# Attention and a two-layer network on one core: the first batch in two blocks of 384 tokens, and a planner that counts VectorE's reads of its own last result

## The chip, the cores and the metric

The kernel runs on one core of a Trainium2 chip. The metric is the device time of one execution in microseconds (us); several executions are timed and their median is given. One further execution is recorded by the profiler. The engines are TensorE (PE), VectorE (DVE), ScalarE (ACT), GpSimd (POOL) and SyncE (SP), which issues the DMAs. Each runs its own instructions in the order in which they stand in the program and waits for the others at semaphores.

## The reference

```python
# q, k, v: (4 batches, 8 heads, 768 positions, 64); 8 global keys, a local window of 96
scores = scale * np.matmul(q, k.transpose(0, 1, 3, 2)) + bias   # bias falls with the distance, by head
scores = np.where(is_global | is_local, scores, -1e9)
a = softmax(scores)                                             # with 1e-9 added to the sum
x = np.matmul(a, v)                                             # -> 3072 tokens x 512
h = x @ w_in                                                    # 512 x 2048
out = (h * np.cos(h)) @ w_out                                   # 2048 x 512
```

All of q, k and v are float32; the two weights are float64 and come as pairs of 32-bit words that the kernel turns into two float32 parts, a high one and a rest.

## The kernel before, in words

Attention goes by blocks of 96 queries (R), which need 96 + 104 keys each. The 8 blocks of a batch are taken as chunks of 3, 3 and 2 (BLOCKS), so there are 12 chunks in all. A chunk has four units, one for each pair of heads. A unit's scores are made on PE (line 632 in plain float32 for the first 8 units, which the code calls exact; line 636 from a high part and a rest, split on ACT, POOL and DVE, for the others), masked and reduced on DVE (fold, line 654; least, line 663), put through exp on ACT (line 688), scaled (lines 712 and 717), turned on PE (line 803), copied out of PSUM with two masks (lines 814 and 820), and multiplied with v (line 846). The result is split into xh and xl (lines 269, 271 and 893).

The network goes by chunks m of 256 tokens (MW). A step is one chunk with two of the 16 slices f of 128 hidden columns: m1 (line 909, function moe1) makes 128 x 256 of h for each slice, so that one elementwise pass is 512 wide: turns on ACT (927), angle on DVE (930), cosine on ACT (933), product on DVE (966), then high (269) and rest (977). m2 multiplies with w_out about 2.6 steps later: chunks 0 to 3 plainly (line 922, moe2), chunks 4 to 11 (m of FAST or more) with seven instead of eight products (line 1071), whose sums of g are four DVE or POOL instructions in one piece of work (lines 1017 to 1020). The weights are decoded once, slice by slice, while the first chunks run (lines 407 to 438; wjoin is 428, the rest is 438). PHASES says how far the first chunk goes before the second one starts.

The order on every engine is made by a planner (class Plan): every piece of work is an op with a cost on each engine that may do it, a due time, and the buffers it uses (named places of which each class has a few); the planner walks through time, takes the op that is due first of those that are ready, and the instructions are written in that order. WEIGHT and HURRY say how dear an engine counts when an op may go to several. Where PE would stand idle early on, emit puts in matmuls on zeros (line 1354).

Of the kernel before, what the change touches and what calls it, by code (L numbers as in the profile page):

```python
# [28 lines left out]
WIN = R + SLOT  # L29
BLOCKS = ((0, 1, 2), (3, 4, 5), (6, 7))  # L30
CT = 3
CW = CT * R
MW = 256
# [3 lines left out]
QK = KW + CW  # L37
BIG = 1.0e30
# [7 lines left out]
PERIOD = 6800  # L46
LAG = 2.6
MARGIN, EACH = 1.9, 1.7
# [6 lines left out]
NT, NST, NPV, NX, NV, NRAW, NQK, NRR, NG, NS, NOO = 4, 3, 3, 3, 3, 3, 2, 3, 2, 2, 2  # L55

EXACT = 8
FAST = 4
SUMS = -8

DIFFER = tuple(range(4, 12))
BEFORE = {0: 1000, 1: 10000, 2: -5000}
WLEAD = -2500
SLACK = 350
TAIL = 0.3
# [20 lines left out]
class Op:  # L86
    def __init__(self, engines, emit, after, uses, due, table, extra, port, mode):
        self.engines, self.emit, self.uses, self.due, self.table = engines, emit, uses, due, table
        self.extra, self.port, self.mode = extra, port, mode
        self.slack = 0  # L90
        self.after = [a for a in after if a is not None]
        self.then = []
        self.left = len(self.after)
        self.ready = 0
        self.start = None


class Plan:
# [6 lines left out]
    TABLE = 1300  # L105
    AHEAD = 5000
    SWITCH = 200

    def __init__(self, places, free):
        self.ops = []  # L110
        self.places = {c: list(v) for c, v in places.items()}
        self.busy = {}
        self.free = dict(free)
        self.port = 0
        self.mode = None

# [21 lines left out]
    def run(self):  # L138
# [19 lines left out]
        while todo:  # L158
# [5 lines left out]
            while again:  # L164
                again = False
                for e, f in self.free.items():
# [7 lines left out]
                    holds = lambda o, x: x == POOL or (x == DVE and o.port)  # L174
                    for o in ready[e]:
                        if o.ready > t or (best is not None and o.key >= best.key):
                            continue
# [18 lines left out]
                        if ok:  # L196
                            best = o
# [13 lines left out]
                    d = o.engines[e]  # L211
                    if e == ACT and o.table and o.table != table:
# [35 lines left out]
class Net:  # L248
    def __init__(self, ctx, tc, qk, qt, kt, v, lim, w_in, w_out, out):
        self.tc, self.nc = tc, tc.nc  # L250
        self.qk, self.v, self.w_in, self.w_out, self.out = qk, v, w_in, w_out, out
        self.qt, self.kt = qt, kt
        self.lims = lim
        self.B, self.NCH, self.H, self.D, _ = qk.shape
        self.S = v.shape[1]
        self.DF, self.DM = w_out.shape
        self.NP = self.H // 2
# [114 lines left out]
    def plan_weights(self, f):  # L372
# [5 lines left out]
        first = next(s for s, x in enumerate(self.seq) if x[1] == f // 2)  # L378
        wi = int(first * PERIOD) - WLEAD
        wo = int((first + LAG) * PERIOD) - WLEAD  # L380
# [69 lines left out]
    def plan_combined(self, q):  # L450
# [4 lines left out]
        due = int((next(s for s, x in enumerate(self.seq) if x[0] == FAST) + q + SUMS) * PERIOD)  # L455
# [62 lines left out]
    def plan_loads(self, n, b2):  # L518
# [3 lines left out]
        b, c = divmod(n, self.NCH)  # L522
        W = 2 * UB * D
        nb = len(BLOCKS[c])
        t0 = BLOCKS[c][0] * R
        lead = 1 if c == 0 else 0
        vs = Slot("v", lambda i: self.work.tile([SLOT, 1 + CT, W], F32, name="v", tag=i))
        L = dict(n=n, first=c == 0, v=vs, nb=nb)
        src = self.v[b][:, b2 * W : (b2 + 1) * W]
        nt = 1 + nb - lead  # L530
        s = t0 - (1 - lead) * R

        def blocks(e):
            nc.sync.dma_start(vs.tile[:R, lead : lead + nt], src[s : s + nt * R].rearrange("(t p) d -> p t d", p=R))

        def glob(e):
            nc.sync.dma_start(
                vs.tile[R:, lead:nb], src[:G].rearrange("p (t d) -> p t d", t=1).broadcast_to([G, nb - lead, W])
# [21 lines left out]
    def plan_unit(self, L, pr):  # L560
# [7 lines left out]
        b, c = divmod(n, self.NCH)  # L568
        u["hs"] = slice((pr % UB) * P, (pr % UB + 1) * P)
        att = u["att"] = "early" if n == 0 else "wide" if n <= FAST else "att"  # L570
        exact = self.order.index(n) * self.NP + pr < EXACT
# [3 lines left out]
        row = lambda: Slot("raw", lambda i: self.work.tile([P, QK], F32, name="raw", tag=i))  # L575
        if exact:
            raw = row()
            src = self.qk[b, c, 2 * pr : 2 * pr + 2].rearrange("j p w -> (j p) w")

            def load(e):  # L580
                nc.sync.dma_start(raw.tile[:, k0 : KW + wq], src[:, k0 : KW + wq])

            def queries(e):
                x = raw.tile[:, KW : KW + wq]
# [5 lines left out]
            o = p.op({SP: 470}, load, [], [raw], extra=1422 * (KW + wq - k0) // 1000)  # L590
# [3 lines left out]
        else:  # L594
            heads = [
                self.plan_split(row(), self.qk[b, c, 2 * pr + j], k0, k1, wq, self.steepness(2 * pr + j))
                for j in range(2)
# [20 lines left out]
        for job in jobs:  # L618
# [3 lines left out]
            def score(e, pss=pss):  # L622
                for i in range(len(pss[0][1])):
                    for ps, items in pss:
# [5 lines left out]
                        if exact:  # L630
                            z = raw.tile[j * D : (j + 1) * D]
                            nc.tensor.matmul(out, z[:, KW:][:, q0], z[:, k : k + w], start=True, stop=True)
# [91 lines left out]
    def plan_split(self, raw, src, k0, k1, wq, sc):  # L724

        nc, p, D = self.nc, self.plan, self.D
        qk = Slot("qk", lambda i: [
            self.work.tile([P, 2, CW], F32R, name="qs", tag=f"q{i}"),
            self.work.tile([P, KW], F32R, name="ks", tag=f"k{i}"),
        ])  # L730

        def load(e, a):
            nc.sync.dma_start(raw.tile[a : a + D, k0 : KW + wq], src[:, k0 : KW + wq])

        def qhigh(e):
            nc.scalar.activation(qk.tile[0][:, 0, :wq], raw.tile[:, KW : KW + wq], AF.Copy, scale=sc)

        def qrest(e):
            qs = qk.tile[0]
            nc.vector.scalar_tensor_tensor(  # L740
                qs[:, 1, :wq], raw.tile[:, KW : KW + wq], sc, qs.bitcast(F32)[:, 0, :wq],
# [12 lines left out]
        loads = [p.op({SP: 470}, lambda e, a=a: load(e, a), [], [raw], extra=711 * (KW + wq - k0) // 1000) for a in (0, D)]  # L754
# [7 lines left out]
        k = p.op({DVE: 70 + w * 535 // 512, POOL: 100 + w * 1125 // 512}, krest, [k], [raw, qk], port=True)  # L762
        return qk, [q, k]

    def plan_values(self, u):
        nc, p, D = self.nc, self.plan, self.D
        n, pr, hs, vs, tt, nb = u["n"], u["pr"], u["hs"], u["v"], u["tt"], u["nb"]
# [70 lines left out]
        def av(e):  # L838
            for t in range(nb):
                pv = pvs[t // 2].tile  # L840
                lead = u["first"] and t == 0
                for c in (1,) if lead else (0, 1):
                    k = R if c else SLOT
                    for j in range(2):
# [3 lines left out]
                            (vd.tile[:, off + t] if c and not lead and differ else vs.tile[:k, t + c, hs])[:, j * D : (j + 1) * D],  # L848
# [21 lines left out]
        s0 = BLOCKS[n % self.NCH][0] * R  # L870
        for n, pr, _, _, _, off in units:
            s, e = s0, s0 + nb * R
            while s < e:
                c = s // MW
                self.plan_x(n, pr, n - n % self.NCH + c, s - c * MW, px, s - s0 + off * R, min(e, (c + 1) * MW) - s, done)
                s = min(e, (c + 1) * MW)

    def plan_x(self, n, pr, m, at, px, c0, w, done):

        nc, p = self.nc, self.plan  # L880
        if m not in self.x:
            self.x[m] = Slot("x", lambda i: [
                self.work.tile([P, self.NP, MW], F32R, name=nm, tag=f"{nm}{i}") for nm in ("xh", "xl")
            ])
        x = self.x[m]
        a, c = slice(at, at + w), slice(c0, c0 + w)

        def high(e):
            self.copy(e, x.tile[0][:, pr, a], px.tile[:, c])

        def rest(e):
            xh, xl = x.tile
            nc.vector.tensor_tensor(xl[:, pr, a], px.tile[:, c], xh.bitcast(F32)[:, pr, a], op=ALU.subtract)  # L893

        o = self.chain("xh", p.op({ACT: 50 + w * 427 // 512, DVE: 70 + w * 535 // 512}, high, [done], [px, x]))
        self.xdone.setdefault((m, pr), []).append(
            p.op({DVE: 70 + w * 535 // 512}, rest, [o], [px, x], due=self.xdue(n, pr)))

    def xdue(self, n, pr):
        rest = self.NP - 1 - pr  # L900
        first = next(s for s, x in enumerate(self.seq) if x[0] == n)
        if n in EARLY:
            return first * PERIOD - BEFORE[n] - rest * EARLY[n]
        return int((first - MARGIN - rest * EACH) * PERIOD)
# [30 lines left out]
    def plan_step(self, s, m, q, a, b):  # L935

        nc, p = self.nc, self.plan
        due = s * PERIOD
        x = self.x[m]
# [486 lines left out]
```

## Time and profile before

| | before |
|---|---|
| median of 3 runs (lowest to highest) | 693.3 us (692.57 to 694.97) |
| the profiled execution: its time | 693.8 us |
| its span, first to last instruction | 691.9 us |
| PE, DVE, ACT, POOL busy, share of the span | 97%, 83%, 76%, 47% |
| granted TensorE clock, mean | 0.987 |

The profiled execution is 1.9 us longer than its span, which is time around the first and last instruction. Busy time of PE is modelled and holds waits in part, so a PE that is busy 97% need not be at its peak: the pace of its matmuls tells more.

### The profile page before, as it was taken

The page shows a single profiled execution, that of the slowest core. Times are in us where ns is not written, and L with a number is a line of the kernel's source. Part 1 is how long each engine was busy: PE and PEld are TensorE (multiplying, and loading weights), DVE is VectorE, ACT ScalarE, POOL GpSimd, SP SyncE. Part 2 cuts the span into 40 slices and gives each one's busy share as a digit, 9 for nine tenths or more (in the row PEclk, how much of TensorE's full clock was granted, in tenths as well). Part 3 has the DMA queues.
Part 4 walks back from the last instruction along what each step waited for, and adds up shares of the span by engine and source line. Part 5 has one row for each costly group of instructions (what it writes and reads, how often), then busy time and mean ns, then how long its engine had stood idle before and what let it go on. Part 6 is the DMA issues. An engine that isn't in the chain of part 4 may idle for free.

```text
span 691.9 us, 17874 instructions
## 1 busy us (share of the span) xinstructions
PE 668.4 (97%) x5979; PEld 627.0 (91%) x5979; DVE 574.5 (83%) x1813; ACT 525.9 (76%) x1311; POOL 322.5 (47%) x463
## 2 busy tenths in 40 slices
PE   6998999999999999999999999999999999999995
PEld 3677899889999999999999989999999989999995
DVE  6899998999889898888987887877987787887764
ACT  6899997887878868768878877666887786875442
POOL 6682434453445535415455665562545665630200
PEclk8899999999999999999999999999999999999998
DMA  8999000443546666776777767776877966665664
GB/s 290 286 359 347 29 1 1 130 129 115 194 142 200 196 205 202 219 220 213 243 237 219 222 194 216 240 235 220 241 219 218 265 196 203 200 214 182 216 196 157
DMA packets 88053, 138.56 MB, mean 200 GB/s; under 512 B 10256, under 2 KB 34704, under 8 KB 87952
## 3 DMA queue, kind: packets, MB, share of 16 engines
q1 hardware_dynamic: 87952, 137.32, 64.1%
q8 instruction: 50, 0.82, 0.5%
q14 instruction: 51, 0.42, 0.2%
HBM read 120.51 MB, written 16.78 MB: 198 GB/s over the span
## 4 chain that ended last, share of the span: by engine, by line
PE 38%; DVE 24%; ACT 16%; issue 5%; POOL 5%; DMA 2%; SPq 0%; POOLq 0%; DVEq 0%; ACTq 0%
PE bank L909 17%; PE bank L1071 10%; PE bank L922 5%; ACT tt L688 3%; DVE rr L966 2%; PE bank L846 2%; PE bank L636 2%; DVE tt L663 2%; DVE rr L930 2%; ACT rr L933 2%; DVE qs L740 2%; DVE bank L654 2%; ACT sh L269 1%; DVE gl L977 1%; DVE sl L1026 1%
## 5 line engine op out<-in xcount | busy, mean ns | idle before, releaser
L909 PE MATMUL bank<-xh,w 128*128 128x256 f32 x1536 | 329.2, 285 | 0.8 <-DVE rr L966 0.4
L909 PEld LDWEIGHTS bank<-xh,w 128*128 128x128 f32 x1536 | 257.9, 189 | 7.8 <-DVE rr L966 1.6
L909 PE MATMUL bank<-xl,w 128*128 128x256 f32 x768 | 215.2, 280 | 0.0
L909 PEld LDWEIGHTS bank<-xl,w 128*128 128x128 f32 x768 | 145.3, 189 | 2.2 <-DVE xl L893 0.2
L688 ACT ACTIVATE tt<-tt,st 96x104 f32<-96x104 f32 (+1 forms) x256 | 94.6, 371 | 6.4 <-DVE st L663 5.7
L933 ACT ACTIVATE rr<-rr,half_pi 128x512 f32<-128x512 f32 x96 | 69.4, 723 | 28.8 <-DVE rr L930 28.0
L966 DVE TENSOR_TENSOR rr<-bank,rr 128x512 f32<-128x512 f32 x96 | 66.0, 688 | 29.3 <-ACT rr L933 28.9
L922 PE MATMUL bank<-w,gh 128*128 128x256 f32 (+1 forms) x384 | 87.9, 322 | 2.5 <-DVE w L438 1.4
L717 POOL TENSOR_TENSOR tt<-tt,st 96x416 f32<-96x416 f32 (+1 forms) x64 | 45.0, 710 | 77.3 <-DVE qs L740 30.1
L269 ACT CAST gh<-rr 128x384 fp32r<-128x384 f32 (+1 forms) x86 | 46.9, 545 | 40.5 <-DVE rr L966 26.9
L930 DVE SCALAR_TENSOR_TENSOR rr<-rr,bank 128x512 f32<-128x512 int32 x96 | 65.3, 680 | 11.6 <-ACT rr L927 11.1
L1071 PE MATMUL bank<-ws,sh 128*128 128x256 f32 x384 | 72.9, 284 | 0.2
L927 ACT ACTIVATE rr<-bank 128x512 int32<-128x512 f32 x96 | 56.6, 589 | 16.3 <-PE bank L909 15.9
L922 PEld LDWEIGHTS bank<-w,gh 128*128 128x128 f32 x384 | 58.9, 188 | 5.1 <-DVE w L438 2.6
L922 PE MATMUL bank<-w,gl 128*128 128x256 f32 (+1 forms) x192 | 60.9, 317 | 0.0
L636 PE MATMUL bank<-ks,qs 128*96 128x200 f32 (+1 forms) x416 | 56.3, 259 | 3.9 <-DVE st L663 3.1
L269 ACT CAST sh<-sf 128x512 fp32r<-128x512 f32 x57 | 35.4, 620 | 31.0 <-DVE sf L1020 17.0
L1071 PEld LDWEIGHTS bank<-ws,sh 128*128 128x128 f32 x384 | 58.2, 188 | 0.8 <-DVE oo L1089 0.6
L663 DVE CUSTOM_DVE_ANT_0 tt<-bank,dd 96x104 f32<-96x104 f32 (+1 forms) x256 | 56.4, 257 | 2.9
L636 PEld LDWEIGHTS bank<-ks,qs 128*96 128x96 f32 x416 | 46.8, 162 | 8.9 <-issue 5.0
L1071 PE MATMUL bank<-ws,sl 128*128 128x256 f32 x192 | 53.5, 279 | 0.0
L1071 PE MATMUL bank<-w,gh 128*128 128x256 f32 x256 | 48.5, 281 | 0.0
(132 smaller groups left out, 1595.5 us busy)
## 6 DMA issues: line engine op xcount, KB each, us to landing
ws<-sum SPq DMA_DIRECT2D x256, 256.0 KB
raw<-in_qk_dram SPq DMA_DIRECT2D x64, 150.0 KB
raw<-in_qk_dram SPq DMA_DIRECT2D x48, 174.0 KB
raw<-in_w_in_dram SPq DMA_DIRECT2D x16, 512.0 KB
sum<-sw SPq DMA_DIRECT2D x64, 128.0 KB
raw<-in_qk_dram SPq DMA_DIRECT2D x48, 148.0 KB
out_dram<-oo SPq DMA_DIRECT2D x24, 256.0 KB
v<-in_v_dram SPq DMA_DIRECT2D x32, 144.0 KB
```

The source lines that it names most:

```text
L269: self.nc.scalar.copy(out, x)
L636: nc.tensor.matmul(out, qs[:, m, q0], ks[:, k : k + w], start=m == 0, stop=m == 1)
L663: nc.vector.tensor_tensor_reduce(tt[t // 2].tile[:, t % 2, j, :w], ps.tile[:R, i * WIN : i * WIN + w], self.dd[:, v, :w], op0=ALU.add, op1 ...
L688: nc.scalar.activation(x, x, AF.Exp, bias=st.tile[:, c : c + 1], scale=-1.0, accum_out=st.tile[:, n2 + c : n2 + c + 1])
L717: self.eng(e).tensor_tensor(x, x, r.broadcast_to([R, na, SLOT]), op=ALU.mult)
L909: self.nc.tensor.matmul(ph, self.wi[f][:, w, kk * P : (kk + 1) * P], xx[:, kk, :], start=kk == 0 and m == 0, stop=kk == self.NK - 1 and m ...
L922: self.nc.tensor.matmul(out, gg, w[:, i, :], start=start and m == 0 and h == 0, stop=stop and m == 2)
L927: self.nc.scalar.activation(r.bitcast(I32), ph, AF.Copy, scale=1.0 / TWO_PI, bias=0.25)
L930: self.nc.vector.scalar_tensor_tensor(r, r.bitcast(I32), -TWO_PI, ph, op0=ALU.mult, op1=ALU.add)
L933: self.nc.scalar.activation(r, r, AF.Sin, bias=self.half_pi)
L966: {DVE: dve(512)}, lambda e: nc.vector.tensor_tensor(r(), h(), r(), op=ALU.mult), [o], [ph, rr],
L1071: nc.tensor.matmul(out, x, y, start=q == 0 and j == 0 and half == 0, stop=q == self.NF // 2 - 1 and j == 2 and ends)
```

## The change

The first batch (768 tokens) becomes two parts of four blocks, 384 tokens each (OPEN), with units of four query blocks; the other batches keep chunks of 3, 3 and 2 blocks, so there are 11 attention chunks and 44 units instead of 12 and 48. The network takes these two parts as chunks 0 and 1, 384 wide, with one slice f to a step (plan_opening): elementwise work is 384 wide, m2 has three groups of 128 tokens, which take PSUM banks A, B and C. Chunk 0 does slices 0 to 3, chunk 1 all 16, then chunk 0 the other 12. The x of both lies in one memory with the three slots of the later chunks (share, xtile). Chunks from 3 on (FAST) use the seven products, which are again 8 chunks of 256. Since the first 8 units stay exact and have four blocks, two more blocks of each head pair are scored in float32, and 72 instead of 80 heads are split. There are two raw buffers instead of three, and the exact units use the qk buffers too.

The planner now knows that an instruction of DVE or POOL that reads what the one before it on its engine wrote starts later (DRAIN, DEFER), and takes other ready work first. The last of the four sums of the seven products becomes an op of its own, so that something can stand ahead of it. Costs, margins, due times and engine weights have new values.

```diff
+OPEN = ((0, 1, 2, 3), (4, 5, 6, 7))
-CT = 3
+CT = 4
-PERIOD = 6800
-LAG = 2.6
+PERIOD, OPENING = 6800, 5200
+LAG = 18000
-HURRY, HURRY_TO = {PE: 1, ACT: 0.3, DVE: 2, POOL: 0.6}, 50000
-WEIGHT = {PE: 1, ACT: 0.6, DVE: 1.5, POOL: 0.8}
-PHASES = [(0, 0, 4), (1, 0, 8), (0, 4, 8)]
+HURRY, HURRY_TO = {PE: 1, ACT: 0.4, DVE: 1.2, POOL: 0.7}, 160000
+WEIGHT = {PE: 1, ACT: 1, DVE: 1.2, POOL: 0.7}
+PHASES = [(0, 0, 4), (1, 0, 16), (0, 4, 16)]
-FAST = 4
+FAST = 3
-TAIL = 0.3
+TAIL = 0
...
+    DRAIN = 113
+    DEFER = 2000
+    def drained(self, o, e):
+        last = self.last.get(e)
+        return e in (DVE, POOL) and last is not None and (last in o.after or o.apart or last.apart)
...
+                        key = o.key
+                        if self.drained(o, e):
+                            key = (key[0] + self.DEFER * (self.last[e] in o.after), key[1])
...
+                    if self.drained(o, e):
+                        d += max(0, self.DRAIN - (t - f))
+                    self.last[e] = o
...
+    def plan_opening(self, s, m, f, a, b):
+        due = self.when[s]
+        ph = self.bank("ph")
...
+        for kk in range(self.NK):
+            def m1(e, kk=kk):
+                self.moe1(ph.tile[:, :CW], *self.xtile(m), f, kk)
...
+        o = p.op({ACT: act}, lambda e: self.turns(e, r(), h()), [done], [ph, rr])
+        o = p.op({DVE: dve}, lambda e: self.angle(e, r(), h()), [o], [ph, rr])
+        o = p.op({ACT: act + 135}, lambda e: self.cosine(e, r()), [o], [rr], table="sin")
...
+        for t in range(NTOK):
+            def m2(e, t=t):
+                self.moe2(po[t].tile, *(z[:, t * P : (t + 1) * P] for z in gg.tile), f, f == a, f == b)
...
-            v.tensor_tensor(s4, a12, s2, op=ALU.subtract)
-        o = p.op({DVE: 820, POOL: 1690}, sums, [product], [rr, sf], port=True)
+        def fourth(e):
+            self.eng(e).tensor_tensor(at(sf.tile, 3), at(rr.tile, 3), at(sf.tile, 1), op=ALU.subtract)
+        o = p.op({DVE: 610, POOL: 1270}, sums, [product], [rr, sf], port=True)
+        o = p.op({DVE: 205, POOL: 425}, fourth, [o], [rr, sf], port=True)
```

Two places show what this does to the order. The first is PE early on, where chunk 0 starts with m1 while its attention is still under way. Before, this stands there (xh and xl are the two parts of x, raw the queries and keys of an exact unit, pv and v the softmax and the values):

```order
L632 MATMUL bank<-raw 96x200 x6
L846 MATMUL bank<-pv,v 64x96 x10
L909 MATMUL bank<-xh,w 128x256
L909 MATMUL bank<-xl,w 128x256
L909 MATMUL bank<-xh,w 128x256
L632 MATMUL bank<-raw 96x200 x2
L909 MATMUL bank<-xh,w 128x256
```

Now the place reads so (xmem is the memory of both parts of x; 963 is m1, 662 the exact scores, 837 the turning, 880 the product with v):

```order
L963 MATMUL bank<-xmem,w 128x384 x3
L1469 LDWEIGHTS zeros
L1469 MATMUL idle<-zeros 128x512
L880 MATMUL bank<-pv,v 64x96 x14
L662 MATMUL bank<-raw 96x200 x4
L837 MATMUL bank<-ident,tt 104x96 x4
L963 MATMUL bank<-xmem,w 128x384 x9
L880 MATMUL bank<-pv,v 64x96 x14
```

A unit's product with v has 14 matmuls instead of 10, m1 is 384 wide, and the parts of the next attention stand in between in smaller groups. The matmuls on zeros are 41 in all, 25 before.

The second place is DVE at the sums for the seven products, in a late chunk. Before, four of them follow each other (sf is their result, rr the product of line 966):

```order
L966 TENSOR_TENSOR rr<-bank,rr 128x512
L1017 TENSOR_TENSOR sf<-rr 128x128
L1018 TENSOR_TENSOR sf<-rr 128x128
L1019 TENSOR_TENSOR sf<-sf,rr 128x128
L1020 TENSOR_TENSOR sf<-rr,sf 128x128
```

Now the fourth sum (line 1127) has another instruction ahead of it, the copy to the high part (line 298), which was on ACT in most steps:

```order
L1020 TENSOR_TENSOR rr<-bank,rr 128x512
L1122 TENSOR_TENSOR sf<-rr 128x128
L1123 TENSOR_TENSOR sf<-rr 128x128
L1124 TENSOR_TENSOR sf<-sf,rr 128x128
L298 CAST gh<-rr 128x384
L1127 TENSOR_TENSOR sf<-rr,sf 128x128
L1031 TENSOR_TENSOR gl<-rr,gh 128x384
L298 CAST sh<-sf 128x512
```

The fourth sum no longer reads what the instruction just before it wrote, and two copies have come to DVE.

## Rows read from the trace of the kernel before

**Rows 1.** The page: span, and each engine's busy time.

```profile
span 691.9 us, 17874 instructions
PE 668.4 (97%) x5979; PEld 627.0 (91%) x5979; DVE 574.5 (83%) x1813; ACT 525.9 (76%) x1311; POOL 322.5 (47%) x463
```

**Rows 2.** Busy PE, PEld, DVE, ACT, POOL by stretch (us), granted clock, DMA share.

```profile
0.00:72.00 72.00, 62.56 (x514) 46.48 (x514) 61.04 (x257) 62.18 (x190) 42.84 (x79) 0.91 0.94 315
72.00:120.00 48.00, 47.68 (x357) 44.83 (x356) 44.12 (x75) 43.34 (x92) 20.64 (x17) 1.00 0.01 1
120.00:160.00 40.00, 39.05 (x357) 35.49 (x356) 36.70 (x132) 31.32 (x86) 16.11 (x22) 1.00 0.44 126
230.00:620.00 390.00, 384.49 (x3572) 370.54 (x3571) 323.83 (x1053) 302.75 (x755) 201.05 (x292) 1.00 0.73 220
```

**Rows 3.** PE's groups from 0 to 72 us: busy us, mean ns, idle before.

```profile
L922 PE MATMUL bank<-w,gh 128*128 128x256 f32 x24 | 4.7, 286 | 0.6 <-DVE w L438 0.6
L922 PE MATMUL bank<-w,gh 128*128 128x512 f32 x9 | 3.5, 442 | 1.5 <-ACT w L269 1.0 <-DVE w L438 0.5
```

**Rows 4.** PE in order of time: start us, length us, instruction, count.

```profile
44.03 1.35 PE L632 MATMUL bank<-raw 64*96 64x200 f32 x12
45.31 0.82 PE L1354 MATMUL idle<-zeros 128*128 128x512 bf16 x3
...
74.79 0.28 PE L909 MATMUL bank<-xh,w 128*128 128x256 f32 x1
74.91 0.28 PE L909 MATMUL bank<-xl,w 128*128 128x256 f32 x1
...
321.10 0.28 PE L1071 MATMUL bank<-ws,sl 128*128 128x256 f32 x1
321.31 0.55 PE L846 MATMUL bank<-pv,v 96*64 96x96 f32 x8
321.69 0.34 PE L846 MATMUL bank<-pv,vd 96*64 96x96 f32 x4
...
322.29 0.50 PE L1071 MATMUL bank<-ws,sh 128*128 128x256 f32 x2
322.63 0.28 PE L1071 MATMUL bank<-ws,sl 128*128 128x256 f32 x1
```

**Rows 5.** DVE's groups from 0 to 72 us, same columns as rows 3.

```profile
L663 DVE CUSTOM_DVE_ANT_0 tt<-bank,dd 96x104 f32<-96x104 f32 x40 | 8.6, 257 | 0.0
L428 DVE SCALAR_TENSOR_TENSOR wu<-raw 128x512 uint32<-128x512 uint32 x11 | 8.0, 733 | 0.2 <-ACT raw L423 0.2
L654 DVE COPY_PREDICATED bank<-mine,bank 96x96 f32<-96x96 uint32 x24 | 5.0, 253 | 1.5 <-PE bank L632 1.4
L814 DVE SCALAR_TENSOR_TENSOR pv<-own,bank 104x192 f32<-104x192 f32 x12 | 4.2, 346 | 1.0 <-PE bank L803 0.9
...
L438 DVE TENSOR_TENSOR w<-wu,w 128x512 fp32r<-128x512 f32 x5 | 3.5, 700 | 0.1
...
L654 DVE COPY_PREDICATED bank<-mine,bank 96x192 f32<-96x192 uint32 x8 | 2.5, 352 | 0.2 <-PE bank L632 0.2
...
L814 DVE SCALAR_TENSOR_TENSOR pv<-own,bank 104x384 f32<-104x384 f32 x4 | 2.2, 550 | 0.1
```

**Rows 6.** DVE in order of time, around the four sums.

```profile
302.10 0.28 DVE L1018 TENSOR_TENSOR sf<-rr 128x128 f32<-128x128 f32 x1
302.30 0.28 DVE L1019 TENSOR_TENSOR sf<-sf,rr 128x128 f32<-128x128 f32 x1
302.62 0.29 DVE L1020 TENSOR_TENSOR sf<-rr,sf 128x128 f32<-128x128 f32 x1
```

**Rows 7.** DVE's groups over the whole span, two widths of line 977.

```profile
L977 DVE TENSOR_TENSOR gl<-rr,gh 128x384 fp32r<-128x384 f32 x40 | 23.4, 584 | 2.5 <-ACT gh L269 2.0 <-POOL gh L273 0.4
...
L977 DVE TENSOR_TENSOR gl<-rr,gh 128x512 fp32r<-128x512 f32 x26 | 18.2, 699 | 0.6
```

**Rows 8.** What PE waited for from 230 to 620 us: us, times, longest.

```profile
PE bank L636 <- DVE st L663: 3.1, 7, 0.9
```

More of the change, by code (lines that the diff above doesn't have):

```diff
@@ L377, in plan_weights @@
         rows = self.w_out.bitcast(U32)[f * P : (f + 1) * P, :]
-        first = next(s for s, x in enumerate(self.seq) if x[1] == f // 2)
-        wi = int(first * PERIOD) - WLEAD
-        wo = int((first + LAG) * PERIOD) - WLEAD
+        first = next(s for s, x in enumerate(self.seq) if x[1] == f and x[0] < len(OPEN))
+        wi = self.when[first] - WLEAD
+        wo = self.when[first] + LAG - WLEAD
         ends = [self.plan_weight(cols, self.wi, f, f"wi{f}", 512, wi)]
@@ L595, in plan_unit @@
             heads = [
-                self.plan_split(row(), self.qk[b, c, 2 * pr + j], k0, k1, wq, self.steepness(2 * pr + j))
-                for j in range(2)
+                self.plan_split(source[2 * pr + j], k0, k1, wq, self.steepness(2 * pr + j)) for j in range(2)
             ]
@@ L631, in score @@
                             z = raw.tile[j * D : (j + 1) * D]
-                            nc.tensor.matmul(out, z[:, KW:][:, q0], z[:, k : k + w], start=True, stop=True)
+                            nc.tensor.matmul(out, z[:, kw:][:, q0], z[:, k : k + w], start=True, stop=True)
                             continue
@@ L752, in krest @@
             )
-        loads = [p.op({SP: 470}, lambda e, a=a: load(e, a), [], [raw], extra=711 * (KW + wq - k0) // 1000) for a in (0, D)]
+        loads = [p.op({SP: 470}, lambda e, a=a: load(e, a), [], [raw], extra=711 * (KS + wq - k0) // 1000) for a in (0, D)]
         w = k1 - k0
@@ L847, in av @@
                             px.tile[j * D : (j + 1) * D, (off + t) * R : (off + t + 1) * R],
-                            (vd.tile[:, off + t] if c and not lead and differ else vs.tile[:k, t + c, hs])[:, j * D : (j + 1) * D],
+                            (vd.tile[:, off + t] if c and not lead and differ else vs.tile[:k, t + c - low, hs])[:, j * D : (j + 1) * D],
                             pv[:k, c, o : o + R],
@@ L869, in plan_values @@
         done.slack = SLACK if n not in EARLY else 0
-        s0 = BLOCKS[n % self.NCH][0] * R
+        if n < len(OPEN):
+            self.plan_x(n, pr, n, 0, px, 0, CW, done)
+            return
+        b, blocks = self.parts[n]
+        s0 = b * self.S + blocks[0] * R
         for n, pr, _, _, _, off in units:
@@ L880, in plan_x @@
         nc, p = self.nc, self.plan
[L881 to L885, printed above, removed]
+        xs = self.xs(m)
         a, c = slice(at, at + w), slice(c0, c0 + w)
         def high(e):
-            self.copy(e, x.tile[0][:, pr, a], px.tile[:, c])
+            self.copy(e, self.xtile(m)[0][:, pr, a], px.tile[:, c])
         def rest(e):
-            xh, xl = x.tile
+            xh, xl = self.xtile(m)
@@ new lines, in xs, with xtile @@
+    def xs(self, m):
+        if m not in self.x:
+            if m < len(OPEN):
+                self.x[m] = self.share[m : m + 2]
+            else:
+                self.x[m] = [Slot("x", None)]
+        return self.x[m]
+    def xtile(self, m):
+        n = CW if m < len(OPEN) else MW
+        a = m * 2 * self.NP * CW if m < len(OPEN) else int(self.x[m][0].at[1:]) * 2 * self.NP * MW
+        x = self.xmem[:, a : a + 2 * self.NP * n].rearrange("p (z k w) -> p z k w", z=2, k=self.NP)
+        return x[:, 0], x[:, 1]
@@ L899, in xdue, with begin @@
+    def begin(self, m):
+        return self.when[next(s for s, x in enumerate(self.seq) if x[0] == m)]
     def xdue(self, n, pr):
         rest = self.NP - 1 - pr
-        first = next(s for s, x in enumerate(self.seq) if x[0] == n)
         if n in EARLY:
-            return first * PERIOD - BEFORE[n] - rest * EARLY[n]
-        return int((first - MARGIN - rest * EACH) * PERIOD)
+            return self.begin(n) - BEFORE[n] - rest * EARLY[n]
+        return self.begin(n) - int((MARGIN + rest * EACH) * PERIOD)
@@ L1116, in plan_store @@
         else:
-            cls = ("oo" if m == 1 else "late") if keep else "wu" if m < FAST else "oo"
+            cls = "part" if keep else "wu" if m < FAST else "oo"
             oo = Slot(cls, lambda i: self.work.tile([P, 512], F32, name="oo", tag=i))
@@ L1319, in windows @@
         self.seq = [(n, i, a, b - 1) for n, a, b in phases for i in range(a, b)]
+        self.when = [0]
+        for n, *_ in self.seq:
+            self.when.append(self.when[-1] + (OPENING if n < len(OPEN) else PERIOD))
+        self.when.pop()
+        self.xmem = self.const.tile([P, NX * 2 * self.NP * MW], F32R, name="xmem")
+        self.share = [Slot(c, None) for c in ("x0", "x1", "x2")]
         for n in self.order:
```

195 lines of the change are left out of this document (125 added, 70 removed).

## Prediction

> **What bounds the kernel now.** First the page. PE is busy 668.4 of 691.9 us, DVE 574.5 [rows 1]: over the whole run TensorE is the limit. Then the busy time by stretch, which tells where it is not. From 72 to 120 us PE is busy 47.68 of 48 us, although DVE is busy 44.12 of them. From 230 to 620 us it is busy 384.49 of 390. From 0 to 72 us it is busy only 62.56 of 72, at a granted clock of 0.91, while DVE has 61.04 and ACT 62.18 [rows 2]. PE's groups of that stretch name the late ones: m2 waits for weights that ACT and DVE are still decoding, 1.5 us at its wide form and 0.6 at the other [rows 3]. The timeline shows how little real work PE has there: behind twelve score matmuls stand three on zeros [rows 4], which count as busy. So the opening is set by how fast DVE and ACT bring the first attention and the first weights, and later stretches by PE, but for a few short waits.
>
> What PE computes does not change: the same tokens, slices and products. One m1 takes 0.12 us from start to start at 256 columns [rows 4]; I take the pace by column as equal at 384, so 0.18. A gain can then come only out of time that PE loses, a loss only by adding to it.
>
> **Opening.** By the written order, the last matmul that PE holds for DVE before the smooth stretch is behind the 121st m1 of 256 before, and behind the 68th of 384 now. What stands ahead of it on either engine is counted in the order and priced by rows, as busy time over count.
>
> DVE, in us. Two more blocks for each of the 8 units: 16 reductions of 8.6/40 = 0.215, +3.4; 16 masked folds go from 96 to 192 wide, 5.0/24 = 0.21 to 2.5/8 = 0.31, and 16 masked copies from 192 to 384 wide, 4.2/12 = 0.35 to 2.2/4 = 0.55 (the two kinds of line taken alike): +1.6 and +3.2 [rows 5]. Weights: one slice in a step of 384 columns instead of two in a step of 512 means that fewer must be ready there. wjoin goes from 11 wide and 6 half to 7 and 4, at 8.0/11 = 0.73 and half of it: -3.7. The rest of the weight goes from 5 wide and 6 half to 3 wide, at 3.5/5 = 0.70 and half of it: -3.5 [rows 5]. Elementwise: 11 passes of 0.70 become 10 of 0.58, by the two widths of the rest of g: -1.9 [rows 7]. Four scalings of the softmax come from another engine, about 0.3 each by the width (estimate from rows 5), +1.2, and the pieces of x are fewer, -0.4. In sum -0.1: DVE gets there as late as before, though with another mix.
>
> PE, in us, by then. m1: 121 of 0.12 become 68 of 0.18, -2.3. m2: 66 pieces of 256 columns become 42, -2.9. Exact scores: 8 more pairs of blocks, four matmul records each, at (45.31 - 44.03)/12 = 0.107: +3.4. Products with v and turnings: 96 more records at (321.69 - 321.31)/8 = 0.0475: +4.6 [rows 4]. In sum PE has 2.8 us more behind it at the same moment, so that much less is left to do once DVE no longer holds it. First term: **-2.8 -0.1, taken as -2.9**. Its bounds: all of the waits on weights and more zeros could go, and DVE's idle 11 us of 72 [rows 2] could shrink by 3, so -6; or the 384-wide first loads and a third more attention before the first step cost that idle time again, so +2.
>
> **Change-overs.** At a burst with v PE loses time on both sides: the m2 ahead of it takes 321.31 - 321.10 = 0.21 instead of 0.12, the one behind it (322.63 - 322.29) - 0.12 = 0.22 [rows 4]. That is 0.2 us a burst, and 44 units instead of 48 are two bursts fewer, since the two-block units share one. Each unit also has its turnings and its scores; I take 0.2 for these together by the same rows. 2 x 0.2 + 4 x 0.2 = 1.2: **-1**, bounds -2 and 0.
>
> **Fewer heads to split, fewer pieces of x.** 72 instead of 80 heads are split, and this work lies from 120 us on. There DVE is busy 36.70 of 40 us and PE idle 0.95 [rows 2]. Some 7 us less DVE work by 160 us takes most of this idle time: **-0.8**, bounds -1 and 0.
>
> **The order of the later stretch.** A sum that reads what the instruction before it wrote starts at 302.62, 0.04 after that one's end at 302.58; the sum ahead, which also reads an earlier result, starts at 302.30, 0.08 before the end at 302.38 [rows 6]. So an adjacent read costs 0.12 more. In the order such pairs go from 254 to 172, 82 x 0.12 = 9.8 us of DVE. Against it stand some 60 more instructions on DVE, chiefly copies to high parts; 60 x 0.58 = 35 us is their upper bound, by the rest of g at 384 [rows 7], and half of it is nearer, as many are narrower. DVE has 66 us free from 230 to 620 us [rows 2], which hides both. What PE loses there in waits is 5.5 us at most, of which 3.1 are seven waits for the reduction on DVE [rows 2, 8]; a planner that is right about 0.12 us moves some of these: **-0.5**, bounds -5 (all go, with those of the stretches beside) and +7 (below).
>
> A page speaks against this part. The Trainium skill, page "VectorE: DVE Perf Modes", section "The DRAIN you can't avoid", says that after each operation the next waits for the pipe to empty, that this happens however operations are chained, and that one should keep their number low; it adds itself that "a next op that is not held starts earlier". By its first sentence the reordering would give nothing and the 60 instructions would be pure cost. This case's trace shows starts ahead of the end [rows 6], so I go by the row; in time the two readings differ by that half microsecond, as long as DVE has room.
>
> Free of cost: the shared memory for x and the loss of one raw buffer (one unit is still loaded ahead, and the DMA share is 0.73 from 230 us on, [rows 2]); if that cover fails, scores wait at the head of a unit, which is in the +7. The end after the last matmul is not touched.
>
> **Sum.** 693.8 is the profiled execution; -2.9 -1 -0.8 -0.5 = -5.2 gives 688.6. The runs' median is 0.5 lower: **688.1 us**. Between the small bounds (-6 -2 -1 -1 and +2) this forecast's own range is 684 to 692.
>
> **Rivals.** *The later waits go too.* Fewer units, fewer drains and corrected costs might take nearly all that PE idles from 120 us to the end: 0.95 in 40 and 5.51 in 390 us, over 560 us some 8 us, of which 1.3 are in my sum. That leaves up to 5 more with some remainder: 683. For it: the longest of these waits are on DVE [rows 8]. Against: waits are planned apart from what the chip does, and seven in 390 us are hard to aim at.
>
> *The opening doesn't come earlier.* 384-wide blocks need four instead of three blocks of scores, softmax and product before the first m1. If DVE idles in place of the weight work that went, the first term is 0 to +2, and the other terms leave 692 to 693.5: 692.7. For it: more matmuls on zeros (41 for 25) are placed early, which says that the planner itself sees longer gaps. Against: they are in front of the first step, when there is nothing else.
>
> *VectorE gets too full (the other side).* It has 83% in the long stretch, 323.83 of 390 [rows 2]. With 35 us of copies and none of the drains' gain it would have 90%, and its answers to PE come later. If this doubles PE's waits from 160 to 680 us (5.5/390 x 520 = 7.3 us), the profiled time is 688.6 + 7.3 = 695.9, the median 695.4, and 697 if the opening fails as well. It decides from the point at which DVE's share passes that of 72 to 120 us, 92% [rows 2], where PE still lost only 0.32 us; that row is what speaks against it.
>
> **How the numbers follow.** Chances: forecast 0.52, later waits too 0.16, opening as late 0.18, DVE too full 0.14. A change of 0.3%, 2.1 us, is about the least that a measurement of this kernel can tell from none, so faster is below 691.2 and slower above 695.4. The forecast lies below 691.2 in nearly all its range (0.48 of 0.52), the second wholly, the third at its lower end (0.03): faster 0.67. Same: 0.04, 0.14 and 0.03 from the fourth: 0.21. Slower: 0.12. For 8 in 10 the range reaches down to 682, below the second case's 683 by the first one's unknown, and up to 695.5, which leaves out the worse half of the fourth.
>
> **What the changed profile would show.** Opening: m1 of 384 with a pace of 0.18 us (if it is 0.19 or more, PE's work grows by 1% of its m1 in the first batch, and the sum shrinks); m2's waits for weights below 2.1 us; PE's last wait for DVE some 3 us earlier for the same work. From 120 to 160 us, PE idle near 0.2. From 230 us on, DVE at 83 to 88%, the wait for the reduction at 2 us or less; if it is 6 or more, the fourth case holds. The fourth sum starts before the end of what is ahead of it. The prediction is wrong if the opening's gain is there and comes back as waits later, or if PE in the opening idles for first blocks rather than for weights.

## The result

The new kernel takes 684.48 us (median of 4 runs, 683.93 to 685.94); the kernel before, measured with it, 694.13 us. The ratio is 0.9864, with a 95% interval from 0.9834 to 0.9894: 9.6 us faster, where 5.2 were forecast. Measured a second time, beside other runs, it is 685.27 against 694.64 us, 0.9879 (0.9857 to 0.9902).

The page of the new kernel, span and busy time, answers to [rows 1]:

```profile
span 682.9 us, 17381 instructions
PE 664.2 (97%) x5803; PEld 627.9 (92%) x5803; DVE 594.3 (87%) x1873; ACT 500.6 (73%) x1241; POOL 313.2 (46%) x440
```

The same stretches as in [rows 2]; the columns are busy PE, PEld, DVE, ACT, POOL, the granted clock and the DMA share:

```profile
0.00:72.00 72.00, 63.67 (x580) 47.47 (x581) 63.69 (x269) 61.86 (x201) 52.04 (x85) 0.95 0.91 314
72.00:120.00 48.00, 48.00 (x294) 45.57 (x293) 43.47 (x79) 43.75 (x96) 22.40 (x22) 1.00 0.09 21
120.00:160.00 40.00, 40.00 (x271) 38.04 (x270) 35.33 (x101) 28.52 (x66) 16.09 (x19) 1.00 0.27 88
...
230.00:620.00 390.00, 387.60 (x3629) 377.34 (x3628) 344.49 (x1115) 289.64 (x708) 178.76 (x262) 1.00 0.75 219
```

PE is now busy throughout from 72 to 160 us, and its idle time from 230 to 620 us falls from 5.5 to 2.4 us, while DVE's share there rises from 83% to 88%. In the first 72 us DVE's idle time falls from 11.0 to 8.3 us, and the mean granted clock rises from 0.91 to 0.95.

Where the time went is seen best at one mark: the first m1 of the token 768, the start of the second batch. It is the same work in both programs. The timeline of PE in the kernel before, at that mark and at its last matmul (start us, length us, instruction):

```profile
200.99 0.40 PE L922 MATMUL bank<-w,gl 128*128 128x512 f32 x1
201.23 0.28 PE L909 MATMUL bank<-xh,w 128*128 128x256 f32 x1
...
684.54 0.28 PE L1071 MATMUL bank<-ws,gl 128*128 128x256 f32 x1
```

And of the new kernel, with a stretch of m1 at 384 columns ahead:

```profile
75.34 4.37 PE L963 MATMUL bank<-xmem,w 128*128 128x384 f32 x24
79.55 0.40 PE L976 MATMUL bank<-w,gh 128*128 128x256 f32 x2
...
191.79 0.49 PE L837 MATMUL bank<-ident,tt 96*96 96x96 f32 x4
192.06 0.60 PE L963 MATMUL bank<-xmem,w 128*128 128x256 f32 x3
...
674.85 0.28 PE L1179 MATMUL bank<-ws,gl 128*128 128x256 f32 x1
```

The mark comes 9.2 us earlier (192.06 for 201.23). From it to the start of the last matmul the two take nearly the same: 674.85 - 192.06 = 482.8 us and 684.54 - 201.23 = 483.3. Read so, the first batch made nearly all of the gain. The matmul records ahead of the mark are not quite the same, though: in the kernel before, 20 more products with v, 2 more turnings and three more m2 of 512 columns are done by then. At the start-to-start paces of the timelines (0.0475 us for a product with v, [rows 4]; 0.07 for a turning and 0.24 for such an m2, from the lines above) the new kernel has about 1.8 us more left to do at its mark. With the work evened out the first batch gains 7.4 us and the rest 2.3.

### The profile page after: what moved, and what is told of

Its sections match the earlier page's. It is cut to its first block, busy times and chain, and to the rows that moved or that the text cites. A ratio compares the mean times of both kernels' runs of the same rounds, so it can differ in the third digit from the quotient of the medians.

```text
span 682.9 us, 17381 instructions
## 1 busy us (share of the span) xinstructions
PE 664.2 (97%) x5803; PEld 627.9 (92%) x5803; DVE 594.3 (87%) x1873; ACT 500.6 (73%) x1241; POOL 313.2 (46%) x440
## 4 chain that ended last, share of the span: by engine, by line
PE 75%; DVE 12%; ACT 6%; DMA 2%; POOL 2%; issue 2%; SPq 1%; POOLq 0%; ACTq 0%; DVEq 0%
PE bank L963 33%; PE bank L1179 18%; PE bank L976 12%; PE bank L880 4%; PE bank L666 4%; PE bank L837 2%; DVE oo L1197 2%; ACT tt L718 2%; DMA raw<-in_qk_dram 1%; DVE tt L693 1%; DVE bank L684 1%; ACT L987 1%; ACT L718 1%; DVE rr L1020 1%; DVE xmem L928 1%
## 5 line engine op out<-in xcount | busy, mean ns | idle before, releaser
L963 PE MATMUL bank<-xmem,w 128*128 128x256 f32 (+1 forms) x2112 | 330.1, 294 | 0.2
L963 PEld LDWEIGHTS bank<-xmem,w 128*128 128x128 f32 x2112 | 290.5, 188 | 6.6 <-DVE rr L1020 0.8
L987 ACT ACTIVATE rr<-rr,half_pi 128x512 f32<-128x512 f32 (+1 forms) x104 | 71.8, 692 | 36.9 <-DVE rr L984 36.1
L981 ACT ACTIVATE rr<-bank 128x512 int32<-128x512 f32 (+1 forms) x104 | 58.0, 559 | 33.8 <-PE bank L963 33.6
L984 DVE SCALAR_TENSOR_TENSOR rr<-rr,bank 128x512 f32<-128x512 int32 (+1 forms) x104 | 66.2, 638 | 11.0 <-ACT rr L981 10.5
L1020 DVE TENSOR_TENSOR rr<-bank,rr 128x512 f32<-128x512 f32 x72 | 49.3, 685 | 16.9 <-ACT rr L987 16.8
L296 ACT CAST gh<-rr 128x384 fp32r<-128x384 f32 (+1 forms) x73 | 37.9, 519 | 26.0 <-DVE rr L1020 19.3
L666 PE MATMUL bank<-qk 128*96 128x200 f32 (+1 forms) x384 | 50.2, 257 | 0.8 <-DVE st L693 0.4
L444 POOL TENSOR_SCALAR raw<-raw 128x512 bf16<-128x512 bf16 (+1 forms) x31 | 34.9, 1157 | 33.9 <-DVE w L465 17.1
L718 ACT ACTIVATION_READ_ACCUMULATOR tt<-tt,st 96x1 f32 x256 | 48.1, 188 | 0.0
```

The costliest lines, as they stand in the source:

```text
L296: self.nc.scalar.copy(out, x)
L666: nc.tensor.matmul(out, qs[:, m, q0], ks[:, k : k + w], start=m == 0, stop=m == 1)
L718: nc.scalar.activation(x, x, AF.Exp, bias=st.tile[:, c : c + 1], scale=-1.0, accum_out=st.tile[:, n2 + c : n2 + c + 1])
L963: self.nc.tensor.matmul(ph, self.wi[f][:, w, kk * P : (kk + 1) * P], xx[:, kk, :], start=kk == 0 and m == 0, stop=kk == self.NK - 1 and m ...
L981: self.nc.scalar.activation(r.bitcast(I32), ph, AF.Copy, scale=1.0 / TWO_PI, bias=0.25)
L984: self.nc.vector.scalar_tensor_tensor(r, r.bitcast(I32), -TWO_PI, ph, op0=ALU.mult, op1=ALU.add)
```

## The experiments

In the table, "mark" is the first m1 of the second batch and "rest" the time from it to the start of the last matmul, both from PE's timeline of the profiled run. e1 to e4, e5 to e8 and e9 to e12 were each measured on one chip, beside runs of the kernel before, to which the ratio refers. Mark and rest come from a single run each: two profiles of the same kernel (new and e9) differ by 0.8 us in the mark and by 1.4 in the rest, and smaller differences are not read. Those on zeros aside, the matmuls done by the mark are the same by count in before, e3 and e11, and the same but for two turnings in new, e1, e2, e9, e10 and e12, so within each of these groups the marks compare.

| run | median us | ratio to before (95%) | mark | rest |
|---|---|---|---|---|
| before | 694.13 | | 201.23 | 483.3 |
| new | 684.48 | 0.9864 (0.9834 to 0.9894) | 192.06 | 482.8 |
| e1 no rule | 693.01 | 0.9993 (0.9975 to 1.0011) | 195.06 | 487.5 |
| e2 old weights | 682.25 | 0.9836 (0.9812 to 0.9859) | 193.71 | 480.8 |
| e3 before with the rule | 694.44 | 1.0011 (0.9994 to 1.0028) | 206.06 | 477.8 |
| e4 fourth sum back | 687.02 | 0.9910 (0.9886 to 0.9935) | 191.97 | 484.0 |
| e5 before, zeros | 693.76 | 0.9999 (0.9986 to 1.0013) | 200.66 | 484.3 |
| e6 new, zeros | 686.69 | 0.9891 (0.9872 to 0.9910) | 194.85 | 482.9 |
| e7 new, loaded | 686.38 | 0.9892 (0.9872 to 0.9913) | 194.03 | 482.6 |
| e8 before, loaded | 698.73 | 1.0061 (1.0040 to 1.0082) | 204.35 | 485.1 |
| e9 new again | 685.27 | 0.9879 (0.9857 to 0.9902) | 192.85 | 481.4 |
| e10 opening alone | 697.82 | 1.0044 (1.0028 to 1.0061) | 196.95 | 491.1 |
| e11 before, rule late | 693.45 | 1.0003 (0.9982 to 1.0023) | 199.49 | 482.8 |
| e12 mixed weights | 680.55 | 0.9805 (0.9784 to 0.9826) | 191.32 | 479.4 |

The theory that I began with: the opening in blocks of 384 makes most of the gain, and the planner's rule on VectorE's reads little, because VectorE has room. The rival: the rule makes it.

**e1, the rule off.**

```diff
-        return e in (DVE, POOL) and last is not None and (last in o.after or o.apart or last.apart)
+        return False
```

> The new kernel with the planner told nothing of VectorE's reads of its own last result (no added time, no deferring; the fourth sum stays an op of its own, and the order is planned anew). Theory: the opening in two blocks of 384 makes most of the 9.6 us, so 684.5 to 686.5 us. Rival: the gain comes from the planner's new rule, so 688 to 692 us.

693.01 us, no faster than before: even beyond the rival's range. The mark is still 6.2 us earlier than before, 195.06, so the opening keeps two thirds of its gain; but the rest takes 487.5 instead of 482.8 us. What PE waited for from 230 to 620 us in this run (us in all, times, longest):

```profile
PE bank L666 <- DVE st L693: 1.5, 4, 0.5
PE bank L666 <- POOL qk L783: 1.3, 3, 0.6
PE bank L963 <- DVE rr L1020: 1.0, 3, 0.5
PE bank L837 <- POOL tt L747: 1.0, 2, 0.6
```

In the new kernel the same view has

```profile
PE bank L1179 <- DVE oo L1197: 1.4, 2, 0.8
PE bank L666 <- DVE st L693: 0.4, 1, 0.4
PE bank L666 <- POOL qk L783: 0.2, 1, 0.2
```

The wait for the reduction, 3.1 us in the kernel before [rows 8], is 0.4 with the rule and 1.5 without it. What the rule did does not show at the fourth sums: of those on VectorE, the ones right behind the third are 35 of 35 in the trace before, 3 of 34 in the new one and only 4 of 45 in e1, since the fourth sum is an op of its own there too. The 4.7 us behind the mark do not come from these. Of all such reads, counted as DVE instructions behind the mark that name the output of the one ahead and start within 0.1 us of its end, e1 has 221 and the new kernel 166; 55 x 0.12 = 6.6 us of DVE, so e1 by itself leaves the reads elsewhere as a possible cause.

**e2, the engine weights of before.**

```diff
-HURRY, HURRY_TO = {PE: 1, ACT: 0.4, DVE: 1.2, POOL: 0.7}, 160000
-WEIGHT = {PE: 1, ACT: 1, DVE: 1.2, POOL: 0.7}
+HURRY, HURRY_TO = {PE: 1, ACT: 0.3, DVE: 2, POOL: 0.6}, 50000
+WEIGHT = {PE: 1, ACT: 0.6, DVE: 1.5, POOL: 0.8}
```

> The new kernel with the engine weights of the kernel before (WEIGHT, HURRY, HURRY_TO). Theory: these only move work between engines that have room, 685 to 688 us, with more copies on ACT again. Rival: the new weights make the gain, 689 to 694 us.

682.25 us: below both ranges. The new weights are not the gain. By the profiles they bring the mark forward by 1.6 us and cost 2.0 us behind it; against e9 it is 0.9 and 0.6, so that the split is no more than a hint. In the stretch from 230 to 620 us DVE is back at 84%, and PE idles 1.75 us:

```profile
230.00:620.00 390.00, 388.25 (x3642) 378.80 (x3641) 327.68 (x1056) 307.71 (x748) 207.05 (x288) 1.00 0.75 222
```

**e3, the rule put into the kernel before.** The lines of the change on DRAIN, DEFER, drained and the fourth sum, and nothing else:

```diff
+    DRAIN = 113
+    DEFER = 2000
...
+                        if self.drained(o, e):
+                            key = (key[0] + self.DEFER * (self.last[e] in o.after), key[1])
...
-        o = p.op({DVE: 820, POOL: 1690}, sums, [product], [rr, sf], port=True)
+        o = p.op({DVE: 610, POOL: 1270}, sums, [product], [rr, sf], port=True)
+        o = p.op({DVE: 205, POOL: 425}, fourth, [o], [rr, sf], port=True)
```

> The kernel before with only the planner's rule on VectorE's reads and the fourth sum as an op of its own. Theory: worth at most 2 us alone, 692 to 694 us. Rival: the rule is the gain, 686 to 690 us.

694.44 us: no gain, which is 0.4 us beyond the theory's range and far from the rival's. The zero is a sum of two: the rest shrinks by 5.5 us, to 477.8, and the mark comes 4.8 us later, at 206.06. In this plan the later stretch gains more than 2 us, and the old opening, planned anew with the rule, loses as much.

**e4, the fourth sum back behind the third, all other instructions in the same order.**

```diff
             v.tensor_tensor(s2, s1, a11, op=ALU.subtract)
+            v.tensor_tensor(at(z, 3), a12, s2, op=ALU.subtract)
...
         def fourth(e):
-            self.eng(e).tensor_tensor(at(sf.tile, 3), at(rr.tile, 3), at(sf.tile, 1), op=ALU.subtract)
+            pass
...
```

> The new kernel in the same order, but the fourth sum stands right behind the third again: 64 adjacent reads at 0.12 us, about 7 us more of DVE in the seven-product stretch. Theory: DVE has room there, so 684.5 to 685.2 us. Rival: the time that TensorE gained in the later stretch, about 2 us, comes from this, so 686.5 us.

687.02 us; the ratio of 0.9910 is 0.0031 to 0.0046 above the two of the new kernel, 2.2 to 3.2 us: the rival's size, though the intervals overlap. Its mark is where it was (191.97), the loss lies behind it (484.0 us). DVE in order of time in the new kernel, around one group of sums:

```profile
299.33 0.28 DVE L1123 TENSOR_TENSOR sf<-rr 128x128 f32<-128x128 f32 x1
299.54 0.28 DVE L1124 TENSOR_TENSOR sf<-sf,rr 128x128 f32<-128x128 f32 x1
299.74 0.35 DVE L298 CAST gh<-rr 128x384 fp32r<-128x384 f32 x1
300.01 0.28 DVE L1127 TENSOR_TENSOR sf<-rr,sf 128x128 f32<-128x128 f32 x1
```

and in e4, where line 1125 is the fourth sum:

```profile
299.61 0.28 DVE L1123 TENSOR_TENSOR sf<-rr 128x128 f32<-128x128 f32 x1
299.81 0.28 DVE L1124 TENSOR_TENSOR sf<-sf,rr 128x128 f32<-128x128 f32 x1
300.13 0.29 DVE L1125 TENSOR_TENSOR sf<-rr,sf 128x128 f32<-128x128 f32 x1
300.34 0.35 DVE L298 CAST gh<-rr 128x384 fp32r<-128x384 f32 x1
```

From the third sum to the fourth it is 0.32 us in e4, from the third sum to the independent copy 0.20 in the new kernel. All 42 fourth sums on DVE in the trace of e4 start that late, 3 of 34 in that of the new kernel: 39 x 0.12 = 4.7 us of DVE. But the edit undoes more than the order. As an op of its own, the fourth sum of the new kernel is on the other of the two engines, DVE or POOL, than the three ahead of it in 32 of 64 cases; in e4 it always follows them, which gives DVE 8 more, 8 x 0.20 = 1.6 us. So e4 tells what the freedom of the fourth sum is worth, in order and in engine, and not the adjacent read alone: of some 6.3 us of DVE, 2.2 to 3.2 reach the end. PE waits 1.5 us for the reduction again:

```profile
PE bank L1180 <- DVE oo L1198: 2.6, 2, 1.3
PE bank L666 <- DVE st L693: 1.5, 4, 0.6
PE bank L837 <- POOL tt L747: 0.2, 1, 0.2
```

**e5, zeros in the kernel before where PE idles from 52 to 60 us**, to see whether the clock of 0.57 behind it costs time.

```diff
-FILL_TO, FILL_REST, FILL_EACH, FILL_FIRST, FILL_COLD = 45000, 150, 250, 10, 7000
+FILL_TO, FILL_REST, FILL_EACH, FILL_FIRST, FILL_COLD = 70000, 150, 250, 10, 7000
```

> The kernel before in the same order, with matmuls on zeros also where TensorE stands idle between 52 and 60 us. Theory: the granted clock of 0.57 from 60 to 64 us follows on that idle time and costs 4 x 0.43 = 1.7 us; with zeros it stays at 1.0, and 692.4 us are measured. Rival: VectorE sets the end of the opening whatever the clock, 693.8 to 694.5 us.

693.76 us: no change, the rival. The stretches of the kernel before

```profile
56.00:60.00 4.00, 2.48 (x15) 1.88 (x15) 3.64 (x9) 3.74 (x11) 1.34 (x1) 1.00 1.03 399
60.00:64.00 4.00, 4.00 (x20) 3.77 (x19) 4.00 (x9) 4.00 (x10) 0.00 (x0) 0.57 1.04 383
```

and of e5

```profile
56.00:60.00 4.00, 3.48 (x20) 2.08 (x19) 3.72 (x9) 3.77 (x10) 1.35 (x1) 1.00 1.03 401
60.00:64.00 4.00, 4.00 (x30) 3.71 (x31) 3.89 (x9) 4.00 (x10) 0.00 (x0) 1.00 1.05 399
```

show that the clock did rise, from 0.57 to 1.00, and that DVE and ACT were as full as ever. The 1.7 us were not on the path: the ratio's interval leaves room for 1.0 us at most.

**e6, the same idea in the new kernel**: 16 matmuls on zeros, into a part of a score bank that nothing reads, while PE waits for the first softmax.

```diff
+                if n > 0 and not free:
...
+                    rows = max(used, key=lambda u: u.end).tile[96:P, :] if used else None
+                    for _ in range(n if used else 0):
+                        nc.tensor.matmul(rows, self.zeros[:, :32], self.zeros.rearrange("p (o w) -> p o w", o=1).broadcast_to([P, 4, P]), start=True, stop=True)
```

> The new kernel in the same order, with 16 matmuls on zeros in the idle stretch before the first turning (about 8.5 to 12.4 us). Theory: if the clock costs time there, the 0.50 from 12 to 16 us and 0.78 from 16 to 20 us rise to 1.0 and give back up to 2.9 us, 681.6 to 683.5 us. Rival: VectorE and ScalarE set the pace there, so 684.5 us, and more if the zeros delay the turning.

686.69 us. The zeros did not run in the idle time: they stood behind a wait of their own and delayed the turning from 12.39 to 16.54 us. In the new kernel and in e6:

```profile
12.39 1.49 PE L837 MATMUL bank<-ident,tt 96*96 96x96 f32 x8 [3.93 <-ACT tt L718]
...
11.58 5.03 PE L1469 MATMUL bank<-zeros 128*32 128x512 bf16 x16 [3.07 <-DVE st L693]
16.54 0.86 PE L837 MATMUL bank<-ident,tt 96*96 96x96 f32 x8
```

The mark came 2.8 us later; by the ratios the end moved by 0.8 to 1.9 us. What a full clock from 12 to 16 us would be worth stays open; what is seen is that part of a 4.2 us delay of the first unit is paid for at the end.

**e7 and e8, more work on DVE in the opening of both kernels**, eight reductions, order unchanged.

```diff
...
             nc.vector.tensor_tensor(self.worst[:R, :n2], self.worst[:R, :n2], st.tile[:, :n2], op=ALU.max)
+            if exact:
+                z = self.zeros.rearrange("p (o w) -> p o w", o=1).broadcast_to([P, 4, P])
+                nc.vector.tensor_reduce(self.pad, z, axis=mybir.AxisListType.X, op=ALU.add)
```

> The new kernel in the same order with one more reduction of 512 values on VectorE in each of the first 8 units, about 0.6 us each, 5 us in all by 57 us. Theory: VectorE still sets the opening, plus 3.5 to 5 us, 688 to 689.5 us. Rival: TensorE or the first blocks set it now, plus 0 to 2 us, 684.5 to 686.5 us.

> The kernel before with the same eight reductions, about 5 us of VectorE by 50 us. Theory: VectorE sets the opening, plus 4 to 5 us, 698 to 699 us. Rival: the loads or ScalarE set it, plus 0 to 2 us, 694 to 696 us.

The load was 5.4 us in each; DVE's groups from 0 to 72 us in e8:

```profile
L683 DVE TENSOR_REDUCE pad<-zeros 128x4 f32<-128x512 bf16 x8 | 5.4, 677 | 0.0
```

The kernel before became 5.2 us slower by the medians on that chip (698.73 for 693.58; 4.2 by the ratio), which is most of the load: DVE sets its opening nearly one to one. Its mark is 3.1 us later and the rest 1.8 us longer, in one profile each. The new kernel is at 0.9892, which is 0.9 to 1.9 us above its two other measurements: DVE does not set the whole of its opening any more, and some 4 us of the load found room.

**e10 and e11, the two parts apart.** e10 is e1 with the weights of e2: the new opening, margins and due times without rule and weights. e11 is e3 with the rule in force only from 130 us of the plan on (shown against e3, without the lines that keep `self.now`):

```diff
-        return e in (DVE, POOL) and last is not None and (last in o.after or o.apart or last.apart)
+        return self.now > 130000 and e in (DVE, POOL) and last is not None and (last in o.after or o.apart or last.apart)
```

> The new kernel with the engine weights of before and without the planner's rule: what is left is the opening in blocks of 384, with the new margins and due times. Theory of two separate gains: the opening alone is worth 4 to 5 us, 689 to 691 us. Rival: the opening gains only together with the rule, 693 to 694.5 us.

> The kernel before with the planner's rule in force only from 130 us of its plan on; the order before that is the old one. Theory of two separate gains: the later stretch loses 5 us less of TensorE, as in the run with the rule throughout, and the opening stays as it was, 688.5 to 690.5 us. Rival: no gain without the new opening, 693 to 694.5 us.

Both miss. e10 takes 697.82 us, slower than before: the mark is 4.3 us earlier, but the rest takes 491.1 us, 7.8 more. e11 takes 693.45, ratio 1.0003: the rest, 482.8 us, is as long as before, where e3 with the same rule in the same kernel had 477.8. So the theory of two gains that add up falls. What the order behind the mark costs varies by 5 us and more from plan to plan, and the opening's gain can be eaten up by it. Four of the runs form a square, the new kernel with and without the rule and with either set of weights: without the rule the ratio is 0.0114 to 0.0129 higher with the new weights (e1 against new and e9) and 0.0208 higher with the old ones (e10 against e2), 8 to 9 and 14 us. But the reads avoided do not sort these runs: by the count used at e1, e10 has 172 behind the mark and e2 169, with a rest that is 10.3 us longer in e10, and e12 below, the fastest of all, has 173. Of the fourth sums on DVE, 14 of 39 stand right behind the third in e10 and 15 of 41 in e12.

**e9 and e12.** e9 is the new kernel beside the three others; e12 keeps the new weights up to 160 us of the plan and has those of before behind that.

```diff
-WEIGHT = {PE: 1, ACT: 1, DVE: 1.2, POOL: 0.7}
+WEIGHT = {PE: 1, ACT: 0.6, DVE: 1.5, POOL: 0.8}
```

> The new kernel once more, beside the three below on one chip: 684 to 685.5 us by every theory.

> The new kernel with its own engine weights up to 160 us of the plan and those of before behind that. Theory: the new weights gain 1.5 us in the first batch and cost 1.9 us later, so 681 to 683 us. Rival: the difference is a matter of single orders, 683.5 to 686 us.

e9 repeats the new kernel. e12 takes 680.55 us, 0.9805 (0.9784 to 0.9826) of before and 4.7 us less than e9 on the same chip, the best version measured, below the range expected of it. PE idles 1.0 us from 230 to 620 us:

```profile
230.00:620.00 390.00, 389.00 (x3658) 379.97 (x3657) 328.65 (x1068) 305.22 (x742) 201.47 (x281) 1.00 0.76 220
```

## Why the prediction was right, and where its sizes were not

The direction, the place and the range held; the sum was 4.4 us too small. 684.5 us is the lower edge of the forecast's own range, nearer to the rival's 683 than to 688.1. Two of the recorded bounds do not follow from their terms: the small bounds give 683.3 to 693.0 (the +2 with the other terms as they stand) and not 684 to 692, and the case of the late opening gives 691.0 to 693.0 and not 692 to 693.5.

**Pace.** m1 at 384 columns takes (79.55 - 75.34)/24 = 0.175 us, as equal pace by column had it (0.18).

**First term, the opening, mis-sized.** Forecast -2.9. The matmul work done by 80 us, an estimate from the records counted in the trace at the start-to-start paces of the timelines, is 49.9 us before and 54.7 now, 53.9 in e9: 4.0 to 4.8 us. The step that was off is "DVE gets there as late as before": its work is the same, but its idle time in 72 us fell by 2.7 us, which stood in the text as the bound of -6 and not in the term. e8 shows that such time counts nearly in full in the kernel before. m2's waits for weights, 2.1 us of idle time [rows 3], are gone. PE's groups of the new kernel from 0 to 72 us, with the idle time in the last column:

```profile
L976 PE MATMUL bank<-w,gh 128*128 128x256 f32 x18 | 3.6, 291 | 0.0
...
L976 PE MATMUL bank<-w,gh 128*128 128x512 f32 x6 | 2.0, 412 | 0.0
```

I suspected the clock, 0.95 for 0.91, of having made the rest; for its dip at 60 us e5 says no. For the one at 12 us nothing was shown.

**Change-overs and splitting, mis-sized.** From 80 us to the mark the forecast was 0.8 and part of the 1, some 1.2 us. The rows give 9.2 - 1.8 - 4.0 to 4.8, so 2.6 to 3.4. Some 1.2 us of this is idle time of PE that went, 0.32 + 0.95 us from 72 to 160 us before [rows 2] and none now, against 0.8 forecast. For the rest, by count, 144 records of the product with v stood in this stretch before and 60 stand there now: with four blocks to a unit all attention of the first batch is done by then, in a time when PE has room, and not, as before, a third chunk of it in a stretch where PE is the limit. I counted the units over the whole run, and not which stretch they left. That this move is the cause is argued from the counts; no run separates it.

**Order of the later stretch, right in size and wrong in reason.** Forecast -0.5 and part of the 1; measured -0.5 by the mark, -2.3 with the work evened out. But that the free 66 us of DVE "hides both" failed: in e4 some 6 us of DVE cost 2 to 3 us of the end at a DVE share of 88%. The small net result is a balance: the rule is worth 4.7 us behind the mark against e1, and the new weights, which put copies on DVE, cost up to 2.0 (e2). I had priced the rule at half a microsecond, and in this kernel it decides whether it is faster at all: with the same opening and no rule, e1 is at 0.9993. So it is in part luck that the sum came out on the right side; what the prediction names as its being wrong, a gain in the opening that comes back later, is what e1 and e10 show. What the rule is worth is not explained by the 0.12 us for each read avoided either, since plans with the same number of such reads are the fastest and the slowest of all (173 in e12, 172 in e10). About half of the differences behind the mark is PE's idle time from 230 to 620 us: against the new kernel 2.7 of 4.7 us in e1, 3.3 of 8.3 in e10, -1.4 of -3.4 in e12. Where the other half lies, and why a plan without the rule takes 4 to 8 us longer there than the old one (e1, e10), is open: the margins and due times are new as well, and they were not undone one by one.

**The rule on the drain.** The Trainium skill, page "VectorE: DVE Perf Modes", section "The DRAIN you can't avoid", has each operation wait for an empty pipe; that does not describe these rows. Among the sums, independent operations start 0.20 us apart at a length of 0.28, as its own remark on operations that are not held allows, and only the reader of the last result waits until 0.04 us behind its end. Whether the engine or the program's own semaphores make it wait was not separated.

**Rivals.** "The later waits go too" half came: PE's idle time from 230 to 620 us fell from 5.5 to 2.4 us, the wait for the reduction from 3.1 to 0.4. "The opening doesn't come earlier" and "VectorE gets too full" did not; DVE's share came out at 88%, the upper end of what was said; e2 and e12, at 84%, are faster, which suggests that less would have been better.

## What to carry to other kernels

When work moves, ask which stretch it leaves and which it joins, and price it there: the attention that moved out of a stretch bound by TensorE into the opening seems to cost less here, though no run separates it. A share of free time on an engine hides nothing by itself: add a known load in one place, in the same order, and see what part of it arrives at the end (e4, e7, e8). Where a planner sets the order, a correction of its costs is part of every other change; undo it alone before crediting the rest, and repeat a plan in several variants, since single orders differ by 5 us and more here. And count in the trace what the correction was meant to change: here the adjacent reads did not sort the fast plans from the slow ones.

## What the runs showed of the hardware

A VectorE instruction that reads the result of the one before it starts 0.12 us later than an independent one (0.32 against 0.20 us from start to start at 128 columns), with a spread of 0.31 to 0.32 over the 42 of e4. A granted clock of 0.57 over 4 us cost nothing that could be measured (e5); DVE and ACT were busy 3.6 to 4.0 of 4 us around it with either clock. Matmuls on zeros into a bank that VectorE was still reading stood 3.07 us behind its reduction in the program as built, although they went to other partitions (e6); whether the program's semaphores or the chip held them was not separated.
